# Pooled attention before an MLP: keys tiled by head pair, the last rows in 32-column matmul tiles, and x of batch 1 turned two steps later

## The chip, the cores and the metric

The kernel runs on one core of one Trainium2 chip. The metric is the device time of one execution in microseconds (us). The profile of a kernel is one execution recorded by the hardware profiler; its span is a little shorter than the time of the same execution (307.3 against 309.05 for the kernel before). Engines are PE (TensorE, matmuls), PEld (its weight loads, which overlap PE), DVE (VectorE), ACT (ScalarE), POOL (GpSimd) and SP (SyncE, which here only issues transfers). PEclk is the clock that the throttle grants TensorE, 1.0 being full speed.

## The reference

Eight batches, eight heads, 576 queries of 64 elements. k and v are averaged over 8 neighbouring rows, so each head has 72 pooled keys. The attention output of all heads becomes x (4608 x 512), which goes through two layers with `h - tanh(h)` between them.

```python
k_p = k.reshape(B, H, Sp, pool, D).mean(axis=3)        # Sp = 576 / 8 = 72
v_p = v.reshape(B, H, Sp, pool, D).mean(axis=3)
scores = scale * np.matmul(q, k_p.transpose(0, 1, 3, 2))
...                                                    # softmax
attn_out = np.matmul(attn, v_p)
x = attn_out.transpose(0, 2, 1, 3).reshape(B * S, H * D)
h = x @ w_in                                           # 512 x 2048
return (h - np.tanh(h)) @ w_out                        # 2048 x 512
```

## The kernel before

The MLP keeps TensorE busy; the attention of the next batch is slipped in between its matmuls. The pooled keys of all heads, 8 x 72 = 576 rows, are cut into four tiles of 128 rows and one of 64. A head pair has 144 rows, so tiles and pairs do not line up: tiles 1, 2 and 3 hold rows of two pairs each, and their scores are two matmuls that add up, one for each pair, with the other pair's columns of `KB` zero.

```python
PAIRS = [[0], [0, 1], [1, 2], [2, 3], [3]]

def scores(b, t):                          # tile t of batch b, in two halves of 288 queries
    ...
    for half in range(2):
        ps = ps_a.tile([128, hs], FP32, name="s_ps", tag="ps_a")
        for n, hp in enumerate(PAIRS[t]):
            nc.tensor.matmul(
                ps[:, :],
                lhsT=KB[b % 2][:, hp * KBW + t * 128 : hp * KBW + (t + 1) * 128],
                rhs=qT[:, hp, half * hs : (half + 1) * hs],
                start=(n == 0), stop=(n == len(PAIRS[t]) - 1),
            )
        nc.scalar.activation(out=E[:, t, half * hs : (half + 1) * hs], in_=ps[:, :],
                             func=ACT.Exp, scale=SCALE)
```

Batch 0 has nothing to hide behind, so its start is arranged by hand. k comes in three transfers (tiles 0 and 1, the 64 rows, tiles 2 and 3) on the queue of SyncE, q in three on the queue of ScalarE. A few matmuls on zeros (`warm_pe`) stand in the gaps.

```python
load_rows(k_rows, k_raw[0], 0, 0, 2)
load_q0(0, 4)
load_rows(k_rows, k_raw[0], 0, 4, 5)       # 64 rows, one transfer
load_rows(k_rows, k_raw[0], 0, 2, 4)       # "the second half of k" below
load_q0(4, 8)
nc.scalar.dma_start(out=t0[:QT, :, R, :], in_=q[0, :, QA:S, :]...)   # q's tail
...
k_turn(0, 2)
...
pool_k(0, nc.vector, 4, 5)
pool_k(0, nc.vector, 2, 4)
...
k_turn(2, 5)
q_pe_transpose(0, (2, 3), "act")
v_pe_pool(0, 3)
scores_wide(0, (2,))
v_pe_pool(3, 5)
scores_wide(0, (3, 4))
```

x of batch 1 is turned (transposed) on TensorE between the steps u of the first group's second layer, one step after it was made:

```python
if u >= 9:
    if pend is not None:
        x_pe_transpose(1, *pend)
        pend = None
    if u <= 13:
        pend = (u - 9, av(1, u - 9, ps_any, False))
```

The softmax here doesn't subtract the row's maximum and nothing guards it: scores larger than these inputs give would overflow.

## Time and profile before

| | before |
|---|---|
| median time, runs | 309.02 us, 3 runs, 308.74 to 309.35 |
| span of the profile, mean granted clock | 307.3 us, 0.998 |
| first reciprocal of batch 0 (the first x reaches VectorE) | 16.00 |
| first matmul with w2 | 36.17 |
| first layer of the second group begins | 57.78 |
| period of a steady batch | 31.74 |
| first layer of the last group but one begins | 248.23 |

The moments are starts in the timeline. The chain of waits, which the prediction reads (start, length, engine, result, line, number of instructions), counts a matmul from the end of the one before, so it has 57.95 where the timeline has 57.78. The moments cut the kernel into four stretches: the start, the first group's second layer, six steady batches, and the rest.

Two more lines of the kernel before: the timeline of its transfer queue and of VectorE. Columns: start, length, engine, line, operation, out<-in, count, and in brackets the idle time before it with what ended it.

```profile
1.95 0.59 SPq L98 DMA_DIRECT2D k_raw<-in_k_dram  x1
...
10.44 0.69 DVE L177 TENSOR_TENSOR k_raw<-k_raw 128x512 f32<-128x512 f32 x1 [1.14 <-DMA k_raw<-in_k_dram]
```

The second half of k of batch 0 is issued at 1.95 us, and VectorE begins to pool it when it has landed, at 10.44.

### The profile page before, as it was taken

The page shows a single profiled execution, that of the slowest core. Times are in us where ns is not written, and L with a number is a line of the kernel's source. Part 1 is how long each engine was busy: PE and PEld are TensorE (multiplying, and loading weights), DVE is VectorE, ACT ScalarE, POOL GpSimd, SP SyncE. Part 2 cuts the span into 40 slices and gives each one's busy share as a digit, 9 for nine tenths or more (in the row PEclk, how much of TensorE's full clock was granted, in tenths as well). Part 3 has the DMA queues.
Part 4 walks back from the last instruction along what each step waited for, and adds up shares of the span by engine and source line. Part 5 has one row for each costly group of instructions (what it writes and reads, how often), then busy time and mean ns, then how long its engine had stood idle before and what let it go on. Part 6 is the DMA issues. An engine that isn't in the chain of part 4 may idle for free.

```text
span 307.3 us, 4716 instructions
## 1 busy us (share of the span) xinstructions
PE 297.7 (97%) x1707; PEld 149.2 (49%) x1707; DVE 159.4 (52%) x350; ACT 148.5 (48%) x289; POOL 123.5 (40%) x91
## 2 busy tenths in 40 slices
PE   7789999999999999999999999999999999999995
PEld 2454455445554455445544554455445544444443
DVE  5658714684348524861577066707472657207700
ACT  1657544466336642665166506651566246226511
POOL 8800996870694019801980079207920000000000
PEclk9999999999999999999999999999999999999999
DMA  7999999849654984498558954894521340011033
GB/s 231 229 213 305 251 188 332 253 102 325 187 108 105 300 230 112 97 271 241 105 111 211 319 113 120 209 293 116 112 60 37 80 99 2 34 68 34 3 65 72
DMA packets 61799, 48.74 MB, mean 159 GB/s; under 512 B 35536, under 2 KB 48656, under 8 KB 61776
## 3 DMA queue, kind: packets, MB, share of 16 engines
q1 hardware_dynamic: 55184, 42.35, 51.5%
q0 software_dynamic: 4848, 4.78, 9.5%
q10 hardware_dynamic: 1744, 1.31, 1.5%
q8 instruction: 13, 0.21, 0.3%
q14 instruction: 10, 0.08, 0.1%
HBM read 36.70 MB, written 9.44 MB: 150 GB/s over the span
## 4 chain that ended last, share of the span: by engine, by line
PE 82%; DMA 10%; POOL 3%; DVE 2%; issue 1%; SPq 0%; ACT 0%; POOLq 0%
PE o_ps L408 37%; PE hT_ps L380 36%; PE s_ps L253 4%; DMA w1b<-in_moe_w_in_dram 4%; PE x_ps L302 4%; DMA k_raw<-in_k_dram 3%; DMA w2b<-in_moe_w_out_dram 2%; DVE x_sb L312 1%; POOL k_raw L177 1%; DMA out_dram<-o_sb 1%; PE s_ps L288 1%; PE kT_ps L222 1%; POOL k_raw L180 0%; DVE rden L311 0%; PE xT_ps L342 0%
## 5 line engine op out<-in xcount | busy, mean ns | idle before, releaser
L408 PE MATMUL o_ps<-w2b,gT 128*128 128x512 bf16 x560 | 135.2, 379 | 0.1
L393 DVE TENSOR_TENSOR gT<-hT_ps,t_sb 128x512 bf16<-128x512 f32 x144 | 98.9, 691 | 59.1 <-ACT t_sb L391 58.3
L380 PE MATMUL hT_ps<-xT,w1b 128*128 128x512 bf16 x576 | 127.1, 379 | 0.9 <-ACT xT L349 0.5
L391 ACT ACTIVATE t_sb<-hT_ps 128x512 f32<-128x512 f32 x144 | 85.6, 597 | 39.2 <-PE hT_ps L380 38.7
L380 PEld LDWEIGHTS <-w1b 128*128 128x128 bf16 x576 | 55.9, 98 | 67.1 <-issue 1.4
L408 PEld LDWEIGHTS <-gT 128*128 128x128 bf16 x560 | 51.7, 98 | 49.6 <-issue 0.2
L417 ACT COPY o_sb<-o_ps 128x512 f32<-128x512 f32 x33 | 19.3, 586 | 75.6 <-PE o_ps L408 75.6
L128 POOL CAST q_bf<-q_raw 128x2048 bf16<-128x2048 f32 x7 | 13.2, 1892 | 79.0 <-DMA q_raw<-in_q_dram 77.9
L311 DVE RECIPROCAL rden<-x_ps 128x4 f32<-128x4 f32 x80 | 14.1, 176 | 59.1 <-PE x_ps L302 58.5
L312 DVE TENSOR_TENSOR x_sb<-x_ps,rden 128x256 bf16<-128x256 f32 x80 | 33.9, 424 | 2.8
L177 POOL TENSOR_TENSOR k_raw<-k_raw 128x1280 f32<-128x1280 f32 x7 | 20.2, 2888 | 18.3 <-DMA k_raw<-in_k_dram 18.3
L260 ACT ACTIVATE E<-s_ps 128x288 bf16<-128x288 f32 x60 | 21.4, 409 | 9.6 <-PE s_ps L253 9.6
L302 PE MATMUL x_ps<-VB,E 128*128 128x130 bf16 (+2 forms) x240 | 21.1, 221 | 0.0
L302 PEld LDWEIGHTS <-E 128*128 128x128 bf16 x240 | 17.1, 98 | 7.8
L196 POOL TENSOR_TENSOR v_raw<-v_raw 128x1280 f32<-128x1280 f32 x7 | 20.3, 2899 | 0.0
L253 PE MATMUL s_ps<-qT,KB 128*128 128x288 bf16 x96 | 16.7, 287 | 0.0
L253 PEld LDWEIGHTS <-KB 128*128 128x128 bf16 x96 | 9.2, 98 | 9.1 <-ACT KB L234 2.6
L205 POOL TENSOR_TENSOR VB<-v_raw,mask 128x960 bf16<-128x960 f32 x7 | 12.6, 1795 | 0.6
L199 POOL TENSOR_TENSOR v_raw<-v_raw 128x640 f32<-128x640 f32 x7 | 10.8, 1540 | 0.6
L180 POOL TENSOR_TENSOR k_raw<-k_raw 128x640 f32<-128x640 f32 x7 | 10.8, 1536 | 0.6
L185 POOL TENSOR_TENSOR kd<-k_raw 128x640 bf16<-128x640 f32 x7 | 10.8, 1539 | 0.5
L479 PE MATMUL warm_ps<-xT 128*128 128x512 bf16 x28 | 9.6, 466 | 1.3 <-DVE warm L500 1.3
(67 smaller groups left out, 107.0 us busy)
## 6 DMA issues: line engine op xcount, KB each, us to landing
k_raw<-in_k_dram SPq DMA_DIRECT2D x7, 1024.0 KB, 6.6
q_raw<-in_q_dram SPq DMA_DIRECT2D x7, 1024.0 KB, 12.7
v_raw<-in_v_dram SPq DMA_DIRECT2D x7, 1024.0 KB, 9.1
out_dram<-o_sb SPq DMA_DIRECT2D x38, 128.0 KB, 2.4
out_dram<-o_sb SPq DMA_DIRECT2D x16, 256.0 KB, 2.7
w1b<-in_moe_w_in_dram POOLq DMA_DIRECT2D x4, 512.0 KB, 12.8
w2b<-in_moe_w_out_dram POOLq DMA_DIRECT2D x4, 512.0 KB, 6.8
k_raw<-in_k_dram SPq DMA_DIRECT2D x2, 512.0 KB, 6.5
```

Of the source, the lines that this page charges most:

```text
L177: first = eng.tensor_tensor(out=r[:, :, 0:4, :], in0=r[:, :, 0:4, :], in1=r[:, :, 4:8, :], op=ALU.add)
L196: eng.tensor_tensor(out=r[:, :, 0:4, :], in0=r[:, :, 0:4, :], in1=r[:, :, 4:8, :], op=ALU.add)
L253: nc.tensor.matmul(ps[:, :], lhsT=KB[b % 2][:, hp * KBW + t * 128 : hp * KBW + (t + 1) * 128], rhs=qT[:, hp, half * hs : (half + 1) * hs], ...
L260: nc.scalar.activation(out=E[:, t, half * hs : (half + 1) * hs], in_=ps[:, :], func=ACT.Exp, scale=SCALE)
L302: nc.tensor.matmul(ps[:, h0 : h0 + s1 - s0, :].rearrange("p h d -> p (h d)"), lhsT=E[:, t, c0 : c0 + 128], rhs=vb[:, t, s0:s1, :].rearrang ...
L311: nc.vector.reciprocal(out=rden[:, :, :], in_=ps[:, :, D:D1])
L312: nc.vector.tensor_tensor(out=x_sb[:, half, :, :], in0=ps[:, :, 0:D], in1=rden[:, :, :].to_broadcast([128, 4, D]), op=ALU.mult,)
L380: nc.tensor.matmul(h_tiles[i][:, :], lhsT=w1b[:, fb, i * 128 : (i + 1) * 128], rhs=xT[:, fb, tok0 : tok0 + TG], start=(fb == 0), stop=(fb ...
L391: nc.scalar.activation(out=t_sb[:, :], in_=h_ps[:, :], func=ACT.Tanh)
L393: nc.vector.tensor_sub(out=gT[:, :], in0=h_ps[:, :], in1=t_sb[:, :])
L408: nc.tensor.matmul(o_ps[:, :], lhsT=gts[i][:, tb * 128 : (tb + 1) * 128], rhs=w2b[:, i, :], start=(i == 0), stop=(i == NHID - 1),)
L417: (nc.vector.tensor_copy if g == 0 and tb % 2 else nc.scalar.copy)(out=o_sb[:, :], in_=o_ps[:, :])
```

## The change

The intent: give each head pair a score tile of its own (its first 128 rows of 144), so that no score tile needs two full matmuls; put the last 16 rows of all four pairs into one more tile, at partitions 0, 32, 64 and 96, and compute it with four matmuls that have only 32 columns of weights and can share a pass of the array. Eight full matmuls for each half of the queries become four full and four narrow ones. And x of batch 1 is turned two steps later, so that TensorE need not wait for it. The core of the diff:

```diff
+PR = 2 * G          # 144 rows of a pair
+LO = PR - 128       # 16 left over
+KP = 160            # columns of KB for a pair
+NM = 4
...
-    def load_rows(src, dst, b, t0, t1):
-        ...
-        return nc.sync.dma_start(out=dst[0:64, 4, :], in_=src[b, 512:576, :])
+    def load_main(src, dst, b, t0, t1):
+        return nc.sync.dma_start(out=dst[:, t0:t1, :], in_=src[b, 0:128, t0:t1, :])
+
+    def load_left(src, dst, b):
+        return [
+            nc.sync.dma_start(out=dst[32 * t : 32 * t + LO, NM, :], in_=src[b, 128:PR, t, :])
+            for t in range(NM)
+        ]
...
-    PAIRS = [[0], [0, 1], [1, 2], [2, 3], [3]]
+    def score_mms(b, t, dst, c0, c1):
+        for m in range(NM) if t == NM else (t,):
+            o = m * KP + (128 if t == NM else 0)
+            w = 32 if t == NM else 128
+            p = 32 * m if t == NM else 0
+            nc.tensor.matmul(
+                dst[p : p + w],
+                lhsT=KB[b % 2][:, o : o + w],
+                rhs=qTs[b][:, m, c0:c1],
+                start=True,
+                stop=True,
+            )
...
-    load_rows(k_rows, k_raw[0], 0, 0, 2)
+    load_main(k_pairs, k_raw[0], 0, 0, 2)
     load_q0(0, 4)
-    load_rows(k_rows, k_raw[0], 0, 4, 5)
-    load_rows(k_rows, k_raw[0], 0, 2, 4)
+    load_left(k_pairs, k_raw[0], 0)
+    load_main(k_pairs, k_raw[0], 0, 2, 4)
     load_q0(4, 8)
...
-    k_turn(2, 5)
+    k_turn_left()
+    k_turn(2, 4)
     q_pe_transpose(0, (2, 3), "act")
-    v_pe_pool(0, 3)
-    scores_wide(0, (2,))
-    v_pe_pool(3, 5)
-    scores_wide(0, (3, 4))
+    v_pe_pool()
+    scores_wide(0, (2, 3, 4))
...
-            if pend is not None:
-                x_pe_transpose(1, *pend)
-                pend = None
+            if u >= 11 and pend:
+                x_pe_transpose(1, *pend.pop(0))
             if u <= 13:
-                pend = (u - 9, av(1, u - 9, ps_any, False))
+                pend.append((u - 9, av(1, u - 9, ps_any, False)))
```

Cut from the diff: the masks and copies of `VB`, the copies into `KB`, the zeroing of `k_raw`'s last tile, which now stands ahead of the loads, the order of the exponentials in `scores`, and the x matmuls, of which the third now writes two runs of 65 columns that are not next to each other.

More of the change, by code (lines that the diff above doesn't have):

```diff
@@ L63 @@
     v_rows = v.rearrange("b h (g j) d -> b (h g) (j d)", j=POOL)
+    k_pairs = k_rows.rearrange("b (t r) n -> b r t n", r=PR)
+    v_pairs = v_rows.rearrange("b (t r) n -> b r t n", r=PR)
     w1b = const.tile([128, NFB, DFF], BF16, name="w1b")
@@ L68 @@
     ident = const.tile([128, 128], BF16, name="ident")
-    mask = const.tile([128, NT, 3, 1], FP32, name="mask")
+    mask = const.tile([128, 3 * NM, 1], FP32, name="mask")
     k_raw = [const.tile([128, NT, POOL * D], FP32, name=f"k_raw{i}") for i in range(2)]
     v_raw = [const.tile([128, NT, POOL * D], FP32, name=f"v_raw{i}") for i in range(2)]
-    KBW = NT * 128
-    STEP = KBW + 2 * G
-    KB = [const.tile([128, NHP * KBW + 2 * G + KBW], BF16, name=f"KB{i}") for i in range(2)]
+    KB = [const.tile([128, NM * KP], BF16, name=f"KB{i}") for i in range(2)]
     q_bf = const.tile([128, R + 1, H, D], BF16, name="q_bf")
     warm = const.tile([128, 1], FP32, name="warm")
-    VB = [const.tile([128, NT, 3, D1], BF16, name=f"VB{i}") for i in range(2)]
+    VB = [const.tile([128, 3 * NM, D1], BF16, name=f"VB{i}") for i in range(2)]
     q_raws = {}
@@ L94, in evac, with load_k, load_v @@
         evac_n[0] += 1
-    def load_rows(src, dst, b, t0, t1):
-        if t1 <= 4:
-            return nc.sync.dma_start(
-                out=dst[:, t0:t1, :],
-                in_=src[b, t0 * 128 : t1 * 128, :].rearrange("(t p) n -> p t n", p=128),
-            )
-        return nc.sync.dma_start(out=dst[0:64, 4, :], in_=src[b, 512:576, :])
-    def load_k(b, cuts=(0, 4, 5)):
-        return [load_rows(k_rows, k_raw[b % 2], b, a, z) for a, z in zip(cuts, cuts[1:])]
-    def load_v(b, cuts=(0, 4, 5)):
-        return [load_rows(v_rows, v_raw[b % 2], b, a, z) for a, z in zip(cuts, cuts[1:])]
+    def load_main(src, dst, b, t0, t1):
[5 more added lines that the diff above has]
+        ]
+    def load_k(b):
+        return [load_main(k_pairs, k_raw[b % 2], b, 0, NM)] + load_left(
+            k_pairs, k_raw[b % 2], b
+        )
+    def load_v(b):
+        return [load_main(v_pairs, v_raw[b % 2], b, 0, NM)] + load_left(
+            v_pairs, v_raw[b % 2], b
+        )
     def load_q(b, nh=1):
@@ L191, in pool_k, with pool_v @@
         return first
-    def pool_v(b, eng, t0=0, t1=NT):
-        r = v_raw[b % 2].rearrange("p t (j d) -> p t j d", d=D)[:, t0:t1, :, :]
-        n = t1 - t0
+    def pool_v(b, eng):
+        r = v_raw[b % 2].rearrange("p t (j d) -> p t j d", d=D)
         eng.tensor_tensor(
@@ L204, in pool_v, with v_spread, kb_main, kb_left @@
         )
-        return eng.tensor_tensor(
-            out=VB[b % 2][:, t0:t1, :, 0:D],
-            in0=r[:, :, 0:1, :].to_broadcast([128, n, 3, D]),
-            in1=mask[:, t0:t1, :, :].to_broadcast([128, n, 3, D]),
-            op=ALU.mult,
+        v_spread(VB[b % 2], r[:, :, 0:1, :], eng)
+    def v_spread(vb, vs, eng):
+        eng.tensor_tensor(
+            out=vb[:, 0 : 2 * NM, 0:D].rearrange("p (t s) d -> p t s d", s=2),
+            in0=vs[:, 0:NM, :, :].to_broadcast([128, NM, 2, D]),
+            in1=mask[:, 0 : 2 * NM, :]
+            .rearrange("p (t s) o -> p t s o", s=2)
+            .to_broadcast([128, NM, 2, D]),
+            op=ALU.mult,
+        )
+        eng.tensor_tensor(
+            out=vb[:, 2 * NM :, 0:D],
+            in0=vs[:, NM, :, :].to_broadcast([128, NM, D]),
+            in1=mask[:, 2 * NM :, :].to_broadcast([128, NM, D]),
+            op=ALU.mult,
+        )
+    def kb_main(kb, ps, t0, t1, engs):
+        kv = kb.rearrange("p (t x) -> p t x", x=KP)
+        engs[0](out=kv[0:D, t0:t1, 0:G], in_=ps[0:D, :, 0:G])
+        engs[1](out=kv[D:128, t0:t1, G:128], in_=ps[D:128, :, G:128])
+    def kb_left(kb, ps, eng):
+        eng(
+            out=kb[D:128, :].rearrange("p (t x) -> p t x", x=KP)[:, :, 128 : 128 + LO],
+            in_=ps[D:128, :].rearrange("p (t x) -> p t x", x=32)[:, :, 0:LO],
+        )
+    def turn_tile(dst, kd, t):
+        nc.tensor.matmul(
+            dst,
+            lhsT=kd[:, t, :, :].rearrange("p a d -> p (a d)"),
+            rhs=ident[:, :],
+            start=True,
+            stop=True,
         )
@@ L213, in k_transpose @@
         kd = kdups.pop(b)
-        kb = KB[b % 2]
-        for half in range(2):
-            ps = alloc([128, 2, 2, G], FP32, "kT_ps")
-            flat = ps.rearrange("p i a g -> p (i a g)")
-            c = half * 4 * G
-            while c < (half + 1) * 4 * G:
-                t = c // 128
-                n = min((t + 1) * 128, (half + 1) * 4 * G) - c
-                nc.tensor.matmul(
-                    flat[:, c - half * 4 * G : c - half * 4 * G + n],
-                    lhsT=kd[:, t, :, :].rearrange("p a d -> p (a d)"),
-                    rhs=ident[:, c - t * 128 : c - t * 128 + n],
-                    start=True,
-                    stop=True,
-                )
-                c += n
-            step = KBW + 2 * G
-            for par, eng in ((0, nc.vector.tensor_copy), (1, nc.scalar.copy)):
-                off = 2 * half * step + par * G
-                pr = slice(par * D, (par + 1) * D)
-                eng(
-                    out=kb[pr, off : off + 2 * step].rearrange("p (i x) -> p i x", x=step)[
-                        :, :, 0:G
-                    ],
-                    in_=ps[pr, :, par, :],
-                )
-    E_tiles = {}
-    PAIRS = [[0], [0, 1], [1, 2], [2, 3], [3]]
+        ps = alloc([128, NM, 128], FP32, "kT_ps")
+        for t in range(NM):
+            turn_tile(ps[:, t, :], kd, t)
+        kb_main(KB[b % 2], ps, 0, NM, (nc.vector.tensor_copy, nc.scalar.copy))
+        ps = alloc([128, 128], FP32, "kT_ps")
+        turn_tile(ps[:, :], kd, NM)
+        kb_left(KB[b % 2], ps, nc.vector.tensor_copy)
+    E_tiles = {}
+    def score_mms(b, t, dst, c0, c1):
[3 more added lines that the diff above has]
+            p = 32 * m if t == NM else 0
+            nc.tensor.matmul(
+                dst[p : p + w],
+                lhsT=KB[b % 2][:, o : o + w],
+                rhs=qTs[b][:, m, c0:c1],
+                start=True,
+                stop=True,
+            )
     def scores(b, t):
@@ L247, in scores @@
         E = E_tiles[b]
-        qT = qTs[b]
         hs = S // 2
+        pss = []
         for half in range(2):
             ps = ps_a.tile([128, hs], FP32, name="s_ps", tag="ps_a")
-            for n, hp in enumerate(PAIRS[t]):
-                nc.tensor.matmul(
-                    ps[:, :],
-                    lhsT=KB[b % 2][:, hp * KBW + t * 128 : hp * KBW + (t + 1) * 128],
-                    rhs=qT[:, hp, half * hs : (half + 1) * hs],
-                    start=(n == 0),
-                    stop=(n == len(PAIRS[t]) - 1),
-                )
+            score_mms(b, t, ps[:, :], half * hs, (half + 1) * hs)
+            pss.append(ps)
+        for half, ps in enumerate(pss):
             nc.scalar.activation(
@@ L262, in scores @@
             )
-    XM = [
-        [(0, 1, 3, 0), (1, 0, 3, 1), (2, 0, 1, 3)],
-        [(2, 1, 3, 0), (3, 0, 3, 1), (4, 0, 1, 3)],
-    ]
     def scores_wide(b, ts):
@@ L284, in scores_tail @@
         )
-    def score_mms(b, t, dst, c0, c1):
-        for n, hp in enumerate(PAIRS[t]):
-            nc.tensor.matmul(
-                dst,
-                lhsT=KB[b % 2][:, hp * KBW + t * 128 : hp * KBW + (t + 1) * 128],
-                rhs=qTs[b][:, hp, c0:c1],
-                start=(n == 0),
-                stop=(n == len(PAIRS[t]) - 1),
-            )
     def av_half(b, blk, half, x_sb, alloc):
@@ L300, in av_half @@
         ps = alloc([128, 4, D1], FP32, "x_ps")
-        for n, (t, s0, s1, h0) in enumerate(XM[half]):
+        for n in range(3):
+            t = 2 * half + n if n < 2 else NM
+            s0 = 2 * t if n < 2 else 2 * NM + 2 * half
             nc.tensor.matmul(
-                ps[:, h0 : h0 + s1 - s0, :].rearrange("p h d -> p (h d)"),
+                ps[:, 2 * n : 2 * n + 2, :].rearrange("p h d -> p (h d)")
+                if n < 2
+                else ps.rearrange("p (a s) d -> p a s d", s=2)[:, :, 1, :],
                 lhsT=E[:, t, c0 : c0 + 128],
-                rhs=vb[:, t, s0:s1, :].rearrange("p h d -> p (h d)"),
+                rhs=vb[:, s0 : s0 + 2, :].rearrange("p h d -> p (h d)")
+                if n < 2
+                else vb[:, s0 : s0 + 2, :],
                 start=(n == 0),
@@ L489, in load_q0 @@
         )
-    load_rows(k_rows, k_raw[0], 0, 0, 2)
+    nc.vector.memset(zeros, 0.0)
+    nc.vector.memset(k_raw[0][:, NM, :], 0.0)
+    load_main(k_pairs, k_raw[0], 0, 0, 2)
     load_q0(0, 4)
-    load_rows(k_rows, k_raw[0], 0, 4, 5)
-    load_rows(k_rows, k_raw[0], 0, 2, 4)
+    load_left(k_pairs, k_raw[0], 0)
+    load_main(k_pairs, k_raw[0], 0, 2, 4)
     load_q0(4, 8)
     nc.scalar.dma_start(out=t0[:QT, :, R, :], in_=q[0, :, QA:S, :].rearrange("h p d -> p h d"))
-    nc.vector.memset(zeros, 0.0)
     warm_pe(13)
@@ L501 @@
     nc.scalar.activation(out=warm[:, :], in_=warm[:, :], func=ACT.Exp)
-    nc.vector.memset(k_raw[0][64:128, 4, :], 0.0)
     nc.vector.memset(KB[0][:, :], 0.0)
     make_identity(nc, ident)
-    nc.gpsimd.memset(v_bf[64:128, 4, :], 0.0)
+    nc.gpsimd.memset(v_bf[:, NM, :], 0.0)
     nc.gpsimd.memset(q_bf[64:128, R, :, :], 0.0)
-    nc.gpsimd.memset(mask[:, :, :, :], 1.0)
-    mflat = mask.rearrange("p t s o -> p t (s o)")
-    nc.gpsimd.affine_select(
-        out=mflat,
-        in_=mflat,
-        compare_op=ALU.is_ge,
-        fill=0.0,
-        base=G,
-        pattern=[[-16, NT], [-G, 3]],
-        channel_multiplier=1,
-    )
-    nc.gpsimd.affine_select(
-        out=mflat,
-        in_=mflat,
-        compare_op=ALU.is_ge,
-        fill=0.0,
-        base=-1,
-        pattern=[[16, NT], [G, 3]],
-        channel_multiplier=-1,
-    )
-    for i in range(2):
-        nc.gpsimd.tensor_scalar_mul(VB[i][:, :, :, D:D1], mask[:, :, :, :], float(POOL))
-    nc.gpsimd.dma_start(
-        out=v_bf[:, 0:3, :], in_=v_rows[0, 0:384, :].rearrange("(t p) n -> p t n", p=128)
-    )
-    nc.gpsimd.dma_start(out=v_bf[:, 3, :], in_=v_rows[0, 384:512, :])
-    nc.gpsimd.dma_start(out=v_bf[0:64, 4, :], in_=v_rows[0, 512:576, :])
+    nc.gpsimd.memset(mask[:, :, :], 1.0)
+    for m, base, step, cm in (
+        (mask[:, 0 : 2 * NM : 2, 0], G - 1, 0, -1),
+        (mask[:, 1 : 2 * NM : 2, 0], -G, 0, 1),
+        (mask[:, 2 * NM :, 0], 0, -32, 1),
+        (mask[:, 2 * NM :, 0], LO - 1, 32, -1),
+    ):
+        nc.gpsimd.affine_select(
+            out=m,
+            in_=m,
+            compare_op=ALU.is_ge,
+            fill=0.0,
+            base=base,
+            pattern=[[step, NM]],
+            channel_multiplier=cm,
+        )
+    for i in range(2):
+        nc.gpsimd.tensor_scalar_mul(VB[i][:, :, D:D1], mask[:, :, :], float(POOL))
+    nc.gpsimd.dma_start(out=v_bf[:, 0:NM, :], in_=v_pairs[0, 0:128, :, :])
+    for t in range(NM):
+        nc.gpsimd.dma_start(
+            out=v_bf[32 * t : 32 * t + LO, NM, :], in_=v_pairs[0, 128:PR, t, :]
+        )
     for c in range(4):
@@ L537 @@
     load_w2(0)
-    nc.gpsimd.memset(k_raw[1][64:128, 4, :], 0.0)
-    nc.gpsimd.memset(v_raw[1][64:128, 4, :], 0.0)
-    nc.gpsimd.memset(v_raw[0][64:128, 4, :], 0.0)
+    nc.gpsimd.memset(k_raw[1][:, NM, :], 0.0)
+    nc.gpsimd.memset(v_raw[1][:, NM, :], 0.0)
+    nc.gpsimd.memset(v_raw[0][:, NM, :], 0.0)
     nc.gpsimd.memset(KB[1][:, :], 0.0)
@@ L547, in k_turn, with k_turn_left @@
     def k_turn(ta, tb):
-        kd = kdups[0]
-        c0, c1 = ta * 128, min(tb * 128, 8 * G)
-        ps = ps_any([128, 512], FP32, "kT_ps")
+        ps = ps_any([128, tb - ta, 128], FP32, "kT_ps")
         for t in range(ta, tb):
-            n = min(128, c1 - t * 128)
-            nc.tensor.matmul(
-                ps[:, t * 128 - c0 : t * 128 - c0 + n],
-                lhsT=kd[:, t, :, :].rearrange("p a d -> p (a d)"),
-                rhs=ident[:, 0:n],
-                start=True,
-                stop=True,
-            )
-        for par in range(2):
-            pr = slice(par * D, (par + 1) * D)
-            whole = [h for h in range(par, 8, 2) if h * G >= c0 and (h + 1) * G <= c1]
-            h = whole[0]
-            n = len(whole)
-            o = (h // 2) * KBW + h * G
-            p = h * G - c0
-            nc.vector.tensor_copy(
-                out=KB[0][pr, o : o + (n - 1) * STEP + G]
-                if n == 1
-                else KB[0][pr, o : o + n * STEP].rearrange("p (i x) -> p i x", x=STEP)[:, :, 0:G],
-                in_=ps[pr, p : p + G]
-                if n == 1
-                else ps[pr, p : p + n * 2 * G].rearrange("p (i x) -> p i x", x=2 * G)[:, :, 0:G],
-            )
-        a, z = (3 * G, c1) if ta == 0 else (c0, 4 * G)
-        o = KBW
-        nc.vector.tensor_copy(out=KB[0][D:128, o + a : o + z], in_=ps[D:128, a - c0 : z - c0])
+            turn_tile(ps[:, t - ta, :], kdups[0], t)
+        kb_main(KB[0], ps, ta, tb, (nc.vector.tensor_copy, nc.vector.tensor_copy))
+    def k_turn_left():
+        ps = ps_any([128, 128], FP32, "kT_ps")
+        turn_tile(ps[:, :], kdups[0], NM)
+        kb_left(KB[0], ps, nc.vector.tensor_copy)
     pool_k(0, nc.vector, 0, 2)
@@ L584, in q_turn, with v_pe_pool @@
         )
-    def v_pe_pool(t0, t1):
-        ps = ps_any([128, t1 - t0, D], FP32, "v_ps")
+    def v_pe_pool():
+        ps = ps_any([128, NT, 1, D], FP32, "v_ps")
         for j in range(POOL):
             nc.tensor.matmul(
-                ps[:, :, :],
+                ps[:, :, 0, :],
                 lhsT=ident[:, :],
-                rhs=v_bf[:, t0:t1, j * D : (j + 1) * D],
+                rhs=v_bf[:, :, j * D : (j + 1) * D],
                 start=(j == 0),
@@ L595, in v_pe_pool @@
             )
-        for s in range(3):
-            nc.vector.tensor_tensor(
-                out=VB[0][:, t0:t1, s, 0:D],
-                in0=ps[:, :, :],
-                in1=mask[:, t0:t1, s, :].to_broadcast([128, t1 - t0, D]),
-                op=ALU.mult,
-            )
+        v_spread(VB[0], ps, nc.vector)
     def ps_b1(shape, dtype, name):
@@ L677 @@
     o_pools = [(ps_o, "o_ps"), (ps_o, "o_ps"), (ps_h, "hT_ps"), (ps_h, "hT_ps")]
-    pend = None
+    pend = []
     for u in range(16):
@@ L696 @@
         if u >= 9:
-            if pend is not None:
-                x_pe_transpose(1, *pend)
-                pend = None
+            if u >= 11 and pend:
+                x_pe_transpose(1, *pend.pop(0))
             if u <= 13:
-                pend = (u - 9, av(1, u - 9, ps_any, False))
+                pend.append((u - 9, av(1, u - 9, ps_any, False)))
     pool_k(2, nc.gpsimd)
```

## The prediction

> **What bounds the kernel now.** I read the page first, then the chain of work that ended last in order of time, then the timeline of single engines where the chain leaves TensorE.
>
> ```profile
> span 307.3 us, 4716 instructions
> PE 297.7 (97%) x1707; PEld 149.2 (49%) x1707; DVE 159.4 (52%) x350; ACT 148.5 (48%) x289; POOL 123.5 (40%) x91
> PEclk9999999999999999999999999999999999999999
> ```
>
> TensorE is busy 97% at full clock and the others half of the time. "Busy" overlaps, so the chain has to say what a matmul costs:
>
> ```profile
> 73.75 0.35 PE s_ps L253 x2
> 74.11 0.86 PE o_ps L408 x4
> 74.97 0.49 PE s_ps L253 x4
> ...
> 79.03 0.24 PE s_ps L253 x2
> ...
> 89.69 13.81 PE hT_ps L380 x64
> ```
>
> 64 matmuls of 512 columns take 13.81 us, so one costs 0.216; four of 288 columns take 0.49, so one costs 0.1225. Both fit the number of columns: in the steady batches (2 to 7) a matmul taken away is its columns' time taken off the end. One batch's scores cost 0.35 + 3 x 0.49 + 0.24 = 2.06 us; the 0.35 holds 0.11 us of waiting for the copies of KB. Six batches make 12.3 us, the 4% that the page gives to this line.
>
> Before 58 us other things bind too:
>
> ```profile
> 14.07 0.46 PEld L589 LDWEIGHTS <-ident 128*128 128x128 bf16 x8 [0.61 <-DMA v_raw<-in_v_dram]
> 16.00 0.18 DVE L311 RECIPROCAL rden<-x_ps 128x4 f32<-128x4 f32 x1 [0.57 <-PE x_ps L302]
> ...
> 34.48 6.03 DMA w2b<-in_moe_w_out_dram
> 40.56 1.02 PE o_ps L408 x4
> ```
>
> The first is TensorE waiting for the last tiles of v of batch 0, the second the first x being normalised. The last two are on the chain: the second part of w2 lands at 40.51, and TensorE, whose work before it ends near 40.35, starts 0.2 us later than it could. Time saved before 40 us is therefore lost at this wait, while time lost there moves the end. This transfer hangs on GpSimd's pooling of k of batch 1, which follows that k's transfer (10.5 us), which follows the second piece of w1; none of it depends on TensorE.
>
> ```profile
> 48.61 1.02 PE L408 MATMUL o_ps<-w2b,gT 128*128 128x512 bf16 x4
> 49.48 0.69 PE L342 MATMUL xT_ps<-ident,x_sb 128*128 128x128 bf16 x4
> 50.00 0.52 PE L302 MATMUL x_ps<-VB,E 128*128 128x130 bf16 x6
> 50.36 1.03 PE L408 MATMUL o_ps<-w2b,gT 128*128 128x512 bf16 x4
> ...
> 56.45 0.22 PE L342 MATMUL xT_ps<-ident,x_sb 128*128 128x64 bf16 x2
> 56.85 0.23 PE L342 MATMUL xT_ps<-ident,x_sb 128*128 128x64 bf16 x2 [0.18 <-DVE x_sb L312]
> 56.92 1.03 PE L408 MATMUL o_ps<-w2b,gT 128*128 128x512 bf16 x4
> ```
>
> Here x of batch 1 is turned. A step lasts 50.36 - 48.61 = 1.75 us though its work is 0.86 + 0.36 + 0.23 (four of 128 columns) = 1.45: the transposes wait for VectorE's x_sb.
>
> **What the Trainium skill says.** "TensorEngine Tiling (Array Packing)", Key Properties: tiles work independently, but changing the tiling mode drains the engine. "TensorE: Matmul & The Clock Gate", Part 3, Measured speedup: three column tiles of 32 with 512 columns ran 2.38 times as fast as one after another, so four are side by side but not free. No tiled matmul is in the trace of before, so it can confirm neither. "PSUM — Partial Sum Buffer", Specifications: an access pattern that isn't contiguous slows matmuls. The third matmul of each x tile now writes two runs of 65 in place of one piece; before has only contiguous ones, at 60 ns each (0.36 / 6). I count on no loss for runs so long.
>
> **The change part by part.**
>
> Scores of batches 2 to 7. Before, eight matmuls per half. After, four full ones and four with 32 columns of weights, which share a pass. t = 0 keeps 0.35, t = 1 to 3 cost 2 x 0.1225 each, 0.735 together. The rest: two passes of 0.1225 = 0.245; a stagger of three issues at 29 ns (the chain has eight 64-column matmuls and one of 512 in 0.45, so 29 ns each) = 0.09; two mode switches. In this trace a 512-column matmul is recorded at 379 ns against its 216 ns of pitch, so 163 ns of its tail are normally hidden; I take that as the estimate for a drain, 0.33 for two. Together 0.66. Sum 0.35 + 0.735 + 0.66 = 1.75 against 2.06: 0.31 saved, **1.9 us in six batches**.
>
> Batch 1. Before, 8 x 0.216 + 8 x 0.029 = 1.96. After, 4 x 0.216 + (0.216 + 0.09 + 0.33) + the tail (4 x 0.029 + 0.03 + 0.09 + 0.33) = 2.07: its last tile and its tail switch modes four times. **0.1 lost.**
>
> x of batch 1 two steps later. Four steps give back 0.29 each; the last, from 55.59 to 56.92, lasts 1.33 and has 0.86 + 0.12 of work, so 0.35. Together 1.5. But the fourth block is now turned just ahead of the last step: ScalarE copies o_sb (0.59), then xT (0.59), about 1.4 us with the handovers, against 0.23 + 0.86 + 0.12 = 1.2 on TensorE before the next group reads it: 0.2 back. **1.3 saved.**
>
> Start, batch 0. The pooling of v becomes one run of eight 320-column matmuls, so all of v must have landed (still near 14.07, as GpSimd issues the loads some 0.6 us later but the queue is full anyway). It costs 8 x 0.135 = 1.08, to 15.15; two full score matmuls to 15.58; the tiled ones with one drain and stagger 0.47, to 16.05; handover 0.16; ScalarE, with three exponentials of about 0.55 apart, ends near 16.8. And every first x tile now needs that last score tile, where before the first half needed tiles 0 to 2. So the first x reaches VectorE near 17.05, against 16.00: 1.05 late. From there to 36 us TensorE is nearly solid, so the delay stays. The scores' tail at 29.75 adds two switches, 0.34. Against it the waits of 0.2 (w2) and 0.2 (kd of batch 1 at 37) vanish. **1.0 lost.** The last rows of k and v now come in four transfers of 16 rows. The second half of k now waits for the first piece of q to land, since the built program keeps at most eight transfers of the hardware queues open; that piece landed at 6.7. Its own landing (10.44) may slip by a microsecond, which v's landing hides.
>
> Transposes of k: six matmuls with 576 columns become five with 640; equal. KB copies: two per engine of 290 and 274 ns become one larger one each plus a small one; the wait of 0.11 stays. GpSimd's VB (1.80 us) becomes two of some 1.45 together; off the path, as are six more issues of 0.52 us per batch on the queue of SyncE, which stands idle 5 us per batch.
>
> Sum: -1.9 + 0.1 - 1.3 + 1.0 = -2.1. **309.0 - 2.1 = 306.9 us.**
>
> **The rivals.**
> The tiles run one after another. Nothing in the profile excludes it; the skill speaks against it. Then the last tile costs 8 x 0.1225 + 0.33 = 1.31, a batch 2.4, and six lose 2.0 in place of gaining 1.9: about 311.
> The switches cost nothing: a batch saves 0.64, six 3.8, batch 1 gains 0.65 more and the start 0.5: 306.9 - 1.9 - 0.65 - 0.5 = 303.9.
> The start binds harder: if k's second half or v lands 1.5 us later still, all of it is on the path: 308.5, and if the idle time before it grows long enough for the clock to fall (the page shows none now), 310. If on the contrary the loads land sooner, the start loses nothing: 306.
> The strided x matmuls take twice their time: each batch has ten of them (five blocks, two halves), so 60 on the path of the six steady batches, and 57 ns more each make 3.4 us: 310. Runs of 65 words speak against it.
>
> **Range and chances.** The terms are small and of both signs; drains (about 1.5 either way) and the start (about 1.5) are the widest. Range 304.0 to 309.6. A gain of 2% needs 302.9, which asks for free switches and a harmless start together: 0.05. A loss of 2% needs 315.2, two rivals at once: 0.02.
>
> **What would show it.** Right: in the steady batches tile t = 4 at about 0.66 us on the chain, the others at 0.245, and a batch period 0.3 under the 31.74 of before (89.69 - 57.95); steps near 1.45 from u = 11 on; the first reciprocal near 17; no wait for w2 at u = 4. Wrong: tiled matmuls 0.12 apart, a period of 31.74 or more, x matmuls over 60 ns apart, or a TensorE wait for w2 that has grown.

## The result, and the profile after

| | before | after |
|---|---|---|
| median time | 309.03 us (4 runs, 308.74 to 309.35) | 311.11 us (4 runs, 310.24 to 311.29) |
| ratio | | 1.0061, interval 1.0040 to 1.0083 |
| span, mean granted clock | 307.3 us, 0.998 | 309.5 us, 0.989 |
| first reciprocal of batch 0 | 16.00 | 21.83 |
| first matmul with w2 | 36.17 | 42.13 |
| first layer of the second group | 57.78 | 61.80 |
| six steady batches | 190.45 | 188.42 |
| from there to the end | 59.10 | 59.29 |

A ratio is the mean time of one kernel's fast runs over that of the other's of the same rounds, so it is not quite the ratio of the medians. The kernel became 0.6% slower; the time lies outside the predicted range of 304.0 to 309.6.

By stretch, after minus before: the start up to the first matmul with w2 +5.96 us; the first group's second layer (61.80 - 42.13 = 19.67 against 57.78 - 36.17 = 21.61) -1.94; six steady batches -2.03; the rest +0.19. The sum is +2.2, the difference of the spans. So the change gained 4.0 us where it was meant to gain, and lost 6.0 before it got there.

The page of the changed kernel (span, busy time of the engines, granted clock in 40 slices of 7.7 us):

```profile
span 309.5 us, 4748 instructions
PE 295.7 (96%) x1692; PEld 144.6 (47%) x1692; DVE 158.8 (51%) x345; ACT 147.2 (48%) x282; POOL 121.1 (39%) x102
PEclk9879999999999999999999999999999999999999
```

TensorE has 2 us less of work and the kernel is still longer, so it must be idle somewhere. Slices two and three show an 8 and a 7 that before did not have: somewhere between 8 and 23 us the clock was cut. The chain of waits says what this stretch hangs on:

```profile
0.81 5.31 DMA q_raw<-in_q_dram
6.14 8.29 DMA k_raw<-in_k_dram
14.46 0.70 DVE k_raw L186
...
17.38 2.13 PE v_ps L582 x8
...
21.83 0.20 DVE rden L329
```

A transfer of k follows a transfer of q, though neither needs the other's data. The timeline of the transfer queue and of TensorE gives the rest:

```profile
1.76 2.19 SPq L105 DMA_DIRECT2D k_raw<-in_k_dram  x4
6.14 0.39 SPq L101 DMA_DIRECT2D k_raw<-in_k_dram  x1
...
16.13 0.40 PE L243 MATMUL kT_ps<-ident,kd 128*128 128x128 bf16 x2 [5.16 <-DVE kd L194]
17.17 2.34 PE L582 MATMUL v_ps<-v_raw,ident 128*128 128x320 bf16 x8
```

The second half of k is issued at 6.14, 4.2 us later than before, and VectorE pools it at 14.46 instead of 10.44. TensorE stands idle for 5.16 us, and after that the eight matmuls that pool v take 2.13 us on the chain, 0.266 each, twice the 0.135 that full speed gives. The windows view shows the clock then (window, length, busy time of PE, PEld, DVE, ACT and POOL with the number of instructions, PEclk, DMA share, GB/s):

```profile
14.00:16.00 2.00, 0.00 (x0) 0.00 (x0) 1.47 (x3) 0.00 (x0) 2.00 (x5) 0.50 1.24 206
16.00:18.00 2.00, 1.87 (x14) 1.53 (x15) 0.88 (x4) 1.01 (x2) 0.48 (x1) 0.50 1.24 206
```

Why does k wait for q? The built program has eight semaphores on which the transfers of these two queues report, and a ninth transfer takes the semaphore of an earlier one, so it first waits for that one to land. Three transfers of q, the first of k and the four of 16 rows make eight; the second half of k is the ninth and waits for q's first piece. In the kernel before it was the sixth, and waited for none. The packed trace names the semaphore of each transfer: in the changed kernel the second half of k waits for number 100 and takes it over, and 100 is that of q's first piece; before it had 106 to itself, and in the run win below 110. This is how the program was built, not a property of the chip.

The steady batches went as meant. The chain shows the period, the timeline the parts of one batch:

```profile
93.36 13.83 PE hT_ps L398 x64
...
124.77 13.83 PE hT_ps L398 x64
```

```profile
77.53 0.34 ACT L234 CAST KB<-kT_ps 64x224 bf16<-64x224 f32 x1 [1.11 <-DVE KB L233]
77.92 0.42 PE L268 MATMUL s_ps<-qT,KB 128*128 128x288 bf16 x2
...
82.46 0.43 PE L268 MATMUL s_ps<-qT,KB 128*32 128x288 bf16 x8
82.82 1.90 PE L426 MATMUL o_ps<-w2b,gT 128*128 128x512 bf16 x8
```

The period is 124.77 - 93.36 = 31.41 against 31.74. The last score tile appears as eight matmuls of form 128*32. The MLP matmuls before it end their issue near 82.36 (81.50 + 4 x 0.216), those after it start at 82.82, so the whole tile with its two switches costs 0.46 us. The first score matmul, at 77.92, waits for ScalarE's copy of `KB`: the MLP matmuls ahead of it are issued by 77.62 (76.76 + 4 x 0.216), so 0.30 us are lost here, where before it was 0.1.

x of batch 1, in the timeline of TensorE:

```profile
56.73 1.03 PE L426 MATMUL o_ps<-w2b,gT 128*128 128x512 bf16 x4
...
58.16 1.03 PE L426 MATMUL o_ps<-w2b,gT 128*128 128x512 bf16 x4
```

A step lasts 1.43 us instead of 1.75, about its own work.

### The profile page after: what moved, and what is told of

Same layout as the page of the kernel before. It is cut to its first block, busy times and chain, and to the rows that moved or that the text cites. A ratio compares the mean times of both kernels' runs of the same rounds, so it can differ in the third digit from the quotient of the medians.

```text
span 309.5 us, 4748 instructions
## 1 busy us (share of the span) xinstructions
PE 295.7 (96%) x1692; PEld 144.6 (47%) x1692; DVE 158.8 (51%) x345; ACT 147.2 (48%) x282; POOL 121.1 (39%) x102
## 4 chain that ended last, share of the span: by engine, by line
PE 85%; DMA 5%; DVE 4%; ACT 3%; issue 0%; SPq 0%
PE hT_ps L398 39%; PE o_ps L426 36%; PE x_ps L316 4%; PE s_ps L268 4%; DMA k_raw<-in_k_dram 3%; DVE gT L411 3%; DMA q_raw<-in_q_dram 2%; ACT t_sb L409 2%; PE xT_ps L360 1%; DMA out_dram<-o_sb 1%; DVE KB L233 1%; PE v_ps L582 1%; ACT KB L234 1%; PE qT_ps L159 1%; ACT E L298 1%
## 5 line engine op out<-in xcount | busy, mean ns | idle before, releaser
L316 PE MATMUL x_ps<-VB,E 128*128 128x130 bf16 x240 | 21.0, 221 | 0.5 <-ACT E L298 0.5
L268 PE MATMUL s_ps<-qT,KB 128*128 128x288 bf16 (+5 forms) x128 | 17.0, 291 | 0.9
L268 PEld LDWEIGHTS <-KB 128*128 128x128 bf16 (+1 forms) x128 | 7.0, 96 | 12.9 <-issue 4.0
L367 ACT CAST xT<-xT_ps 128x256 bf16<-128x256 f32 (+1 forms) x14 | 6.1, 434 | 7.7 <-PE xT_ps L360 7.5
```

The lines of the kernel that those rows point to most:

```text
L268: nc.tensor.matmul(dst[p : p + w], lhsT=KB[b % 2][:, o : o + w], rhs=qTs[b][:, m, c0:c1], start=True, stop=True,)
L316: nc.tensor.matmul(ps[:, 2 * n : 2 * n + 2, :].rearrange("p h d -> p (h d)") if n < 2 else ps.rearrange("p (a s) d -> p a s d", s=2)[:, :, ...
```

## The experiments

The theory: all of the loss comes from the late issue of the second half of k, by its lateness and by the cut clock that the idle TensorE then gets; the other parts of the change are worth what was predicted. Rivals: the loss belongs to the new order of the start's work (v pooled in one piece, every x waiting for the last tile), or to the mode switches of the tiled matmuls, at a moment when nothing else is running on TensorE. The kernels win, split, warm and turn1 ran with the kernel before at 308.83 us; full, kb2, kb2_first and quiet with it at 308.69. All gave correct results.

### win: the changed kernel with the eighth place left free

```diff
-    nc.scalar.dma_start(out=t0[:QT, :, R, :], in_=q[0, :, QA:S, :].rearrange("h p d -> p h d"))
 ...
     q_pe_transpose(0, (0, 1), "act")
+    nc.scalar.dma_start(out=t0[:QT, :, R, :], in_=q[0, :, QA:S, :].rearrange("h p d -> p h d"))
     pool_k(0, nc.vector, 4, 5)
```

Only q's tail moves, which nothing needs until much later. Then the second half of k is the eighth transfer and waits for none.

> The changed kernel with one edit: ScalarE's small load of q's last 64 rows is issued later, so the second half of k of batch 0 is the eighth hardware transfer and no longer waits for the first piece of q. Theory 'slot' (the start is late because the four 16-row transfers use up the eight transfer slots): the second half is issued near 4.0 us in place of 6.1 and lands near 10.5 to 11 in place of 14.4, TensorE's clock stays at 1.0, the first reciprocal comes near 17 to 18 in place of 21.8, time 306 to 307. Rival 'queue' (the second half is late because four issues and a memset stand ahead of it and the other queues take the bandwidth): it lands at 13 or later, time 309.5 or more. Rival 'work' (the start is late because v is pooled in one run and every x needs the last score tile): landing may move, the first reciprocal stays after 19.5.

Measured: 306.57 us (305.84 to 307.32, 4 runs), ratio 0.9924 (0.9902 to 0.9947); span 304.7, clock 1.0. Its timeline (transfer queue, VectorE, TensorE):

```profile
3.72 0.46 SPq L101 DMA_DIRECT2D k_raw<-in_k_dram  x1
...
10.00 0.69 DVE L186 TENSOR_TENSOR k_raw<-k_raw 128x512 f32<-128x512 f32 x1
...
13.16 1.25 PE L581 MATMUL v_ps<-v_raw,ident 128*128 128x320 bf16 x8 [0.77 <-DMA v_raw<-in_v_dram]
...
16.56 0.18 DVE L329 RECIPROCAL rden<-x_ps 128x4 f32<-128x4 f32 x1 [1.02 <-PE x_ps L316]
```

k is issued at 3.72 and used at 10.00, v is again what TensorE waits for, and the first reciprocal is at 16.56, 0.56 later than before. Everything else of the change is still in this kernel. So of the 5.83 us by which the first x was late, 5.27 (21.83 - 16.56) hung on that one wait, and the new order of the start and the tiles together can account for no more than the 0.56 that is left.

### split: the kernel before with the four small transfers alone

```diff
-    load_rows(k_rows, k_raw[0], 0, 4, 5)
+    for i in range(4):
+        nc.sync.dma_start(
+            out=k_raw[0][16 * i : 16 * i + 16, 4, :],
+            in_=k_rows[0, 512 + 16 * i : 528 + 16 * i, :],
+        )
     load_rows(k_rows, k_raw[0], 0, 2, 4)
```

> The kernel before with one edit: the last 64 rows of k of batch 0 are loaded in four transfers of 16 rows in place of one; nothing else of the change. Theory 'slot': the second half of k then waits for q's first piece as in the changed kernel, lands near 14, TensorE idles some 5 us, its clock falls, the first reciprocal comes near 21 in place of 16.0; less the 0.4 us of later waits that this covers the time is 313 to 315 in place of 309.0. Rival 'work' (the lateness comes from the new shape of the work in the changed kernel): no change, 308.5 to 310.

Measured: 314.18 us (313.82 to 315.11, 4 runs), ratio 1.0175 (1.0153 to 1.0198); span 313.4, clock 0.989. The timeline:

```profile
6.29 0.39 SPq L98 DMA_DIRECT2D k_raw<-in_k_dram  x1
...
16.26 0.45 PE L557 MATMUL kT_ps<-ident,kd 128*128 128x128 bf16 x3 [5.73 <-DVE kd L185]
```

The old tiling with nothing but the cut of one transfer loses 5.4 us (314.18 - 308.83). In its profile the first matmul with w2 comes at 42.30, 6.13 us later than before; in the changed kernel it was 5.96. This is the other half of the proof: without the tiles, the same wait costs as much.

### warm: the idle time filled, the lateness kept

```diff
     k_turn_left()
+    warm_pe(22)
     k_turn(2, 4)
```

> The changed kernel with one edit: 22 more idle-filling matmuls on zeros while TensorE waits for the second half of k. Theory: the clock falls to half from 12 to 19 us only because TensorE idles 5.2 us; filled, the eight v matmuls take 135 ns each in place of 267, the first reciprocal comes near 20.0 in place of 21.8, and the time is 309.0 to 309.6 in place of 311.1. Rival (the halved clock costs nothing that another wait would not have cost, e.g. v's landing or ScalarE): 310.5 to 311.3.

Measured: 309.51 us (308.91 to 310.41, 4 runs), ratio 1.0013 (0.9994 to 1.0032); span 308.7, clock 1.0. In the timeline the pooling of v is at full speed again, though k came later still in this run (its pooling began at 15.40):

```profile
17.63 1.25 PE L582 MATMUL v_ps<-v_raw,ident 128*128 128x320 bf16 x8
```

The ratios are compared: 1.0061 - 1.0013 is 0.48%, or 1.5 us, give or take 0.9 by the two intervals. That much of the loss is the cut clock, and the rest is plain lateness. The first reciprocal came at 21.04 and not near 20.0 as expected, because k was later; from the pooling of k it took 5.64 us (21.04 - 15.40) against 7.37 in the changed kernel.

### quiet: the changed kernel with less traffic while k is late

GpSimd's memsets for batch 1 are moved ahead of its load issues, so that v and w1 set out some 2 us later (v is issued at 6.13 instead of 4.17).

```diff
         nc.gpsimd.tensor_scalar_mul(VB[i][:, :, D:D1], mask[:, :, :], float(POOL))
+    nc.gpsimd.memset(k_raw[1][:, NM, :], 0.0)
+    nc.gpsimd.memset(v_raw[1][:, NM, :], 0.0)
+    nc.gpsimd.memset(v_raw[0][:, NM, :], 0.0)
+    nc.gpsimd.memset(KB[1][:, :], 0.0)
     nc.gpsimd.dma_start(out=v_bf[:, 0:NM, :], in_=v_pairs[0, 0:128, :, :])
 ...
     load_w2(0)
-    (the same four memsets)
```

> The changed kernel with one edit: GpSimd clears its four buffers before and not after it issues the loads of v, w1 and w2, so these start 2.3 us later. The late second half of k is issued at 6.1 in both. Theory: it takes 8.3 us, and not the 6.3 of 'win', because by then v and w1 share the transfer engines; with them later it lands at 13.4 or sooner in place of 14.4. Rival (once issued it needs 8 us whatever else runs): 14.2 to 14.7.

Measured: 307.92 us (306.96 to 308.87, 2 runs only), ratio 0.9974 (0.9937 to 1.0011). The timeline:

```profile
6.30 0.39 SPq L101 DMA_DIRECT2D k_raw<-in_k_dram  x1
...
11.09 0.68 DVE L186 TENSOR_TENSOR k_raw<-k_raw 128x512 f32<-128x512 f32 x1
```

Issued as late as in the changed kernel, the transfer lands within 4.8 us instead of 8.3 (8.3 in split and turn1 too, 9.0 in warm). So a late issue costs more than its lateness there because other loads are under way: in the changed kernel v had been issued from 4.17 on, ahead of k's 6.14, and w1 from 7.44. It is one profiled run. This is no full repair: v came later and TensorE waited 1.34 us for it, the clock still fell to between 0.50 and 0.67 from 14 to 18 us, and the first reciprocal was at 19.48.

### turn1: x of batch 1 turned one step later instead of two

```diff
-            if u >= 11 and pend:
+            if u >= 10 and pend:
```

> The changed kernel with one edit: x of batch 1 is turned one step later, as before, in place of two. Theory: the stretch from w2's first matmul to the second group, 19.7 us now and 21.8 before, owes 1.3 to 1.6 us of the difference to the later turn; time 312.3 to 312.9. Rival (the stretch is shorter because of fewer score matmuls and vanished waits): 310.8 to 311.5.

Measured: 312.84 us (312.27 to 313.25, 4 runs), ratio 1.0126 (1.0107 to 1.0145). From the first matmul with w2 to the second group it took 21.11 us (41.76 to 62.87) against 19.67, so the two steps are worth 1.4 us; predicted were 1.3. The timeline shows the old wait again, with four transposes taking 0.69:

```profile
54.56 0.69 PE L360 MATMUL xT_ps<-ident,x_sb 128*128 128x128 bf16 x4
...
55.44 1.03 PE L426 MATMUL o_ps<-w2b,gT 128*128 128x512 bf16 x4
```

The timed difference, 0.65% or 2.0 us, is larger than the traces show, but as above 0.9 us of that is within the noise.

### full: the narrow tiles replaced by full ones

On the base of win: `KB` is made wider and zero padded, and the last score tile is computed by four accumulating matmuls with 128 columns of weights.

```diff
-            w = 32 if t == NM else 128
-            p = 32 * m if t == NM else 0
             nc.tensor.matmul(
-                dst[p : p + w],
-                lhsT=KB[b % 2][:, o : o + w],
+                dst,
+                lhsT=KB[b % 2][:, o : o + 128],
                 rhs=qTs[b][:, m, c0:c1],
-                start=True,
-                stop=True,
+                start=(m == 0 or t < NM),
+                stop=(m == NM - 1 or t < NM),
```

> The run 'win' with one edit: the last score tile is made of four accumulating matmuls with 128 columns of weights (zeros outside the 16 of the pair) in place of four 32-column tiles side by side; the result stays right, no mode is switched. Theory: side by side the eight matmuls of a batch take 0.46 us with both switches, one after another 8 x 0.1225 = 0.98; the batch period goes from 31.40 to about 31.9, six batches lose 3.1 us, batch 1 some 0.3 more; time 309.5 to 310.5 against 306.6. Rival (tiles run one after another as well, or the switches eat the gain): 306 to 307.5.

Measured: 310.38 us (309.58 to 311.12, 4 runs), ratio 1.0053 (1.0028 to 1.0078). The timeline of one steady batch:

```profile
77.63 1.14 PE L266 MATMUL s_ps<-qT,KB 128*128 128x288 bf16 x8
78.61 1.89 PE L424 MATMUL o_ps<-w2b,gT 128*128 128x512 bf16 x8
```

The same eight matmuls cost 78.61 - 77.63 = 0.98 us, eight times 0.1225, against 0.46 for the narrow ones with both switches; the period is 31.91 to 31.96 against 31.40. The narrow tiles therefore do run side by side, which settles the first rival of the prediction. Without them the tiling by head pair is 0.5% slower than the kernel before.

### kb2: the copies of KB cut in two

On the base of win, the transposed keys go into two PSUM tiles (pairs 0 and 1; pairs 2 and 3 with the last rows), so that the copies for the first score tile start sooner.

```diff
-        ps = alloc([128, NM, 128], FP32, "kT_ps")
-        for t in range(NM):
-            turn_tile(ps[:, t, :], kd, t)
-        kb_main(KB[b % 2], ps, 0, NM, (nc.vector.tensor_copy, nc.scalar.copy))
-        ...
+        for t0, t1 in ((0, 2), (2, NM)):
+            ps = alloc([128, 3, 128], FP32, "kT_ps")
+            for t in range(t0, t1):
+                turn_tile(ps[:, t - t0, :], kd, t)
+            ...
+            kb_main(KB[b % 2], ps[:, 0:2, :], t0, t1, (nc.vector.tensor_copy, nc.scalar.copy))
+            ...
```

> The run 'win' with one edit: k is turned into two PSUM pieces (pairs 0 and 1; pairs 2 and 3 with the last rows), so the first score tile waits for two copies of half the size. Theory: TensorE's wait ahead of the first score tile grew from 0.10 us before to 0.30 with the change, because VectorE's copy of all four pairs (0.44) and ScalarE's (0.34) follow one another; with halves it returns to 0.10 or less, 0.2 in each of six batches, 1.2 us: 305.2 to 305.8, period 31.2. Rival (another wait, such as the PSUM buffers, takes its place): 306.4 to 306.8.

Measured: 305.32 us (304.76 to 305.82, 4 runs), ratio 0.9884 (0.9865 to 0.9903). The timeline:

```profile
72.78 1.03 PE L428 MATMUL o_ps<-w2b,gT 128*128 128x512 bf16 x4
73.70 0.42 PE L270 MATMUL s_ps<-qT,KB 128*128 128x288 bf16 x2
```

The four MLP matmuls are issued by 72.78 + 4 x 0.216 = 73.64, so the wait is 0.06 us instead of 0.30, and the period falls to 31.15 to 31.17. Six times 0.24 is 1.4 us; against win the ratio fell by 0.40%, or 1.2 us, give or take 0.9. In its profiled run VectorE could use the second half of k only at 10.82, and the clock fell for a while (windows view):

```profile
14.00:16.00 2.00, 2.00 (x12) 0.73 (x10) 0.73 (x2) 0.49 (x2) 2.00 (x5) 0.55 1.23 199
```

### kb2_first: the last tile's scores first

On the base of kb2, the start computes `scores_wide(0, (4, 2, 3))` instead of `(2, 3, 4)`, since every x needs the last tile, but the first ones don't need tile 3.

> As kb2, and in the start the last score tile is made ahead of tiles 2 and 3. Theory: TensorE's wait of 0.47 us for the exponentials of that tile goes and the first reciprocal comes about 0.8 us sooner than in kb2; but the second part of w2 lands near 41 whatever TensorE does, and TensorE reaches it at 41.1 already, so the time falls by 0.2 us or less against kb2. Rival (w2 is not the bound there): 0.5 to 0.8 us faster than kb2.

Measured: 305.25 us (304.61 to 305.56, 4 runs), ratio 0.9885 (0.9870 to 0.9900), so the same as kb2 within the noise. The first reciprocal is at 16.08 (17.84 in the profile of kb2, which has the cut clock), but TensorE then waits at the second part of w2, which does not depend on it:

```profile
41.16 1.02 PE L428 MATMUL o_ps<-w2b,gT 128*128 128x512 bf16 x4 [0.17 <-DMA w2b<-in_moe_w_out_dram]
```

kb2 and kb2_first beat both kernels, by 1.2% against before.

## Why the prediction was wrong

| Step of the prediction | predicted | changed kernel | win |
|---|---|---|---|
| start, to the first matmul with w2 (1.05 + 0.34) | +1.4 | +5.96 | +0.69 |
| first group's second layer (+0.1 - 1.3, and 0.4 of waits gone) | -1.6 | -1.94 | with the next row |
| six steady batches | -1.9 | -2.03 | -3.58 for both |
| rest | 0 | +0.19 | +0.25 |
| all | -2.1 | +2.2 (spans) | -2.6 (spans) |

**The step that failed** is in the paragraph on the start: "Its own landing (10.44) may slip by a microsecond, which v's landing hides." The prediction had found the wait of k's second half for q's first piece, and had even read from the trace when that piece lands (6.7). The issue was thus to move from 1.95 to about 6.7, and only one microsecond of that was carried into the landing, on the silent assumption that the transfer engines, busy anyway, would deliver it at about the same time. The runs showed the opposite: k landed 4.0 us later (6.14 + 8.29 = 14.43 against 10.44 at the latest), after the last of v (13.65 in this trace), so there was nothing left to hide it. Of two kernels with the same work, win issues it at 3.72 and uses it at 10.00, the changed kernel at 6.14 and 14.46: 2.4 us later at the issue are 4.5 later at the use, because the transfer now competes with v and w1 (quiet: 4.8 us from issue to use instead of 8.3). From the kernel before to win, on the other hand, the issue moved by 1.8 us and the use came no later (10.44 and 10.00), so a delay is not always passed on. Why not here was not tested; win had also moved q's tail out of the way.

**The clock** was named only in a rival, "The start binds harder", at 308.5, or 310 with the clock falling. This rival came true, and its size was too small as well: it supposed 1.5 us beyond the microsecond already allowed, where 3.0 came. The clock's own part can be read in two ways that agree. From the pooling of k to the first reciprocal the changed kernel takes 21.83 - 14.46 = 7.37 us; win takes 6.56, of which 0.77 is waiting for v, so 5.79 of work: 1.6 us are the clock. The run warm, with the gap filled, got 1.5 back.

**The start's work** was 1.05 us later by the sum, and 0.56 in win. That it came out smaller is luck: the sum starts from v's landing near 14.07, and in win TensorE had v at 13.16. From there to the first reciprocal win takes 3.40 us, where the sum has 2.98 (17.05 - 14.07). The term that is short is ScalarE's: the three exponentials begin after the first score matmul, near 15.5 in the sum, and take 1.58 in win, so they end near 17.1 and not at 16.8. The prediction of 306.9 us as a whole is met by win (306.57), which is the changed kernel without that wait.

**The steady batches** came out near the sum (2.03 against 1.9), but two errors cancel. The last tile costs 0.46 instead of 0.66: its eight matmuls are two passes of 0.1225, so 0.21 are left for both switches and the stagger, where 0.42 had been allowed. In its place the first tile costs about 0.55 (0.30 of waiting and two of 0.1225) instead of 0.35, because the wait for `KB`, which "stays" at 0.11 in the prediction, grew to 0.30: one copy of all four pairs (0.44 and 0.34 us, one after the other on two engines) takes longer to have its first columns ready than the two smaller copies did. kb2 shows it: with the copy cut in two the wait is 0.06.

**Batch 1.** The turning two steps later was right (1.4 by turn1, 1.3 predicted). The score tiles cost 1.66 us in this trace against a predicted 2.07, the same overestimate of the switches; so they gained 0.30 where 0.1 was to be lost. Of the 0.4 us of waits that were to vanish only the one for w2 was there: in the timeline of before the matmuls run on past the supposed wait for kd (37.04, right after 36.17 + 4 x 0.216). Together 1.4 + 0.30 + 0.2 make the -1.94.

**The other rivals.** Tiles one after another: excluded by full (0.98 against 0.46). Switches free: half true in size, since 0.21 of 0.42 remained; the longer `KB` wait took that gain away. Strided x matmuls: six took 0.345 us against 0.36 before, no loss.

**When the clock falls.** Why did it fall in kb2, whose longest gap was 1.82 us, and not in win at 1.18? The gap alone does not decide: 1.34 was enough in quiet, 1.44 in the kernel before was not. In the traces the granted clock is cut from 12.89 to 19.72 us in the changed kernel, from 14.19 to 17.60 in kb2 and from 14.68 to 18.09 in quiet, that is for one or two times 3.41 us. In the 3.41 us just before these cuts the windows view has TensorE busy for 1.17, 1.42 and 0.92 us (for 0.00 in split and turn1). If all ten traces are divided in such stretches, laid out from their clock records, every one in which TensorE was busy for 1.42 us or less is followed by a cut, as long as the kernel's matmuls go on, and none with 1.86 or more is. Between the two figures nothing was seen. The stretches lie elsewhere in each run, so the same kernel can be lucky or not: two timed runs of kb2 with a clock of 0.994 took 305.80 and 305.82 us, the two with 1.000 took 304.76 and 304.83.

**What stays open.** Why the second half of k lands as early in win as in the kernel before, though it is issued later, and whether the late landing depends on v alone or on w1 as well.

## What to carry to other kernels

When a change cuts one transfer into several, count the open transfers against the semaphores that the built program has, and look up for each later transfer what it will then wait for; a late issue has to be carried into the landing in full, or more when other loads set out in the meantime, until a trace shows otherwise. A gap before a stretch of dense matmuls can cost twice, as here, by its length and by the clock afterwards, so price both; and judge the clock by how busy TensorE is around the gap, not by the gap alone. When a sum comes out right, check its terms one by one: here a wait that had grown was hiding behind a switch that was cheaper than thought, and it was worth another 0.4%.

## What the Trainium skill lacked or had wrong

- "TensorEngine Tiling (Array Packing)", Key Properties, says that changing the tiling mode drains the engine, but gives no time for it. Here both switches and the stagger of four narrow tiles together cost 0.21 us (0.46 for the tile less two passes of 0.1225).
- "TensorE: Matmul & The Clock Gate", Part 1, What's actually happening, has the clock halve after an idle window of about 3.4 us. Stretches of 3.41 us are what the traces show, but they need not be idle: the clock was halved after stretches in which TensorE was busy for 1.42 us (kb2), 1.17 (the changed kernel, 1.9 us after its last matmul) and 0.92 (quiet), and stayed at 1.0 after 1.86 (turn1), 1.98 (before) and 2.15 (win). A gap under 3.4 us is not safe by itself in these runs.
- "PSUM — Partial Sum Buffer", Specifications, says that any access pattern that isn't contiguous slows matmuls significantly. Two runs of 65 columns cost nothing here: 0.345 us per six matmuls, 0.36 with contiguous ones.
- No page that was read prices a late issue: 2.4 us later at the issue became 4.5 at the use (3.72 to 6.14, 10.00 to 14.46), because other loads had set out in between.
